# A convolution fused with a gated feed-forward layer: building the band from 16-column pieces, and another order of the first steps

## The chip, the cores and the metric

The kernel runs on one core of a Trainium2 chip. The metric is the device time of one execution in microseconds, lower being better. It is the median of several executions of the same program. One further execution was taken with the hardware profiler, and every duration of single instructions comes from that one.

## What is computed

`x` is (8, 4096, 192), the convolution's `weight` is (8, 7), one row of 7 taps for each of 8 heads of 24 columns. Each output row of the convolution is a weighted sum of the row and the six before it (zeros ahead of the first row of each of the 8 sequences), with the taps of a head passed through a softmax. The result, 32768 rows of 192, goes through a gated feed-forward layer.

```python
w = np.exp(weight - np.max(weight, axis=-1, keepdims=True))
w = w / (np.sum(w, axis=-1, keepdims=True) + 1e-09)
x_pad = np.concatenate([np.zeros((B, pad, D)), x], axis=1)      # pad = 6
idx = np.arange(S)[:, None] + np.arange(K)[None, :]             # K = 7
x_unf = x_pad[:, idx, :].reshape(B, S, K, H, group)             # H = 8, group = 24
y = np.einsum('hk,bskhg->bshg', w, x_unf).reshape(B * S, D)
g = y @ w_gate                                                  # (192, 1536)
out = (g / (1 + np.exp(-g))) * (y @ w_val) @ w_out              # (1536, 192)
```

## The kernel before

**Tiling.** The 32768 rows are cut into 64 blocks of 512 rows, and the hidden width of 1536 into 12 chunks of 128. A *step* `n` is one chunk of one block: block `b = n // 12`, chunk `j = n % 12`. There are 768 steps. Four blocks form a unit of 2048 rows, for which the convolution is made at one time.

**One step** (`gate_val`, L537): six products of 64 rows by 128 columns with 512 moving columns, three for `gate` and three for `val`. Gate products use rows 0 to 63 of the array, val products rows 64 to 127, and one of each runs beside the other. ScalarE then takes the silu of `gate` (L554) and VectorE multiplies it with `val` into `h` (L556), of which 15 buffers exist.

**Down projection** (`down`, L561; `slot`, L604). The twelve `h` of a block are multiplied by `w_out` into two accumulators, `acc0` and `acc1`. Each `h` is used by row halves, and the halves swap accumulators between a first and a second pass. The 96 products of a block are divided among four slots: slot 1 (first pass, chunks 0 to 5), slot 2 (second pass over these, then the first pass over chunks 6 to 8), slot 3 (second pass over 6 to 8, first over 9 to 11), slot 4 (second pass over 9 to 11, then the two copies out of the accumulators, L626 and L627, and the store). Slots of block `b` stand behind steps 7 and 10 of the block and 1 and 4 of the next. The first product of a slot waits for `after`, a silu of an earlier step: `silu[n - 2]`. A function `work` can be put between the parts of a slot.

**Convolution.** It is a product with a band matrix. For units from 1 on, `band` (32 rows) is used in `conv_half`; its result goes to DRAM, and blocks are read back transposed (`fetch`). For unit 0, the first four blocks, there is a separate, faster way: `early(e)` (L366) makes 64 small products with the wider band `wide`, and ScalarE and VectorE copy the result to `tme`. Blocks 0 to 2 are then turned on TensorE by `eturn` (L430), 15 transposes against the identity `ident`, and copied to the three `xc` tiles that the steps read. Block 3 takes the way over DRAM (`eout`, `efetch`).

**Constants and the band.** On POOL, `pid` holds each partition's number and `jid` (L184) the column numbers 0 to 127. VectorE makes from them `eye`, 32-column pieces of an identity, `shift`, four pieces that select rows, and, at the end of `make_wide` (L346), `ident`. The softmax of the taps gives `split`, each tap as a high and a low half in fp16. `spread_taps` (L278) brings the taps to the partitions by 16 tiny products, and multiplies them with copies of `eye` to `spread`. `make_wide` (L319) makes `wide` from `shift` and `spread` with four products of 512 columns into two banks, and four copies. `keep_warm` (L640) sends products of zeros with 512 columns through TensorE: seven ahead of the taps, two behind.

**Loads.** `x` and the weights are loaded and cast to fp16 by POOL's queue, in the order of the source: `xe` of block 0 (three loads: the first window without its 6 padding rows, the windows 1 to 5, the second row half), the weights of chunks 0 to 2 and 3 to 7 (three loads each), `xe` of block 1, the weights of chunks 8 to 11, `w_out` in two parts, `xe` of blocks 2 and 3, then `x` of unit 1.

**Order.** Every instruction is put in the order of the source on its own engine by `seq` (L72), also those on POOL that issue loads. The first turn is at L656; then the loop over the steps begins (L660). In it `early(1)` follows step 4, `eturn(1)` step 6, slot 1 of block 0 step 7, slot 2 step 10 with `early(2)` in its middle, slot 3 step 13, slot 4 step 16, `eturn(2)` step 17, and `early(3)` is in slot 1 of block 1, at step 19.

## Time and profile before

| what | value |
|---|---|
| median of three executions | 793.20 us (793.19 to 794.07) |
| the profiled execution | 793.83 us, of which its span is 792.0 us |
| TensorE products, share of the span | 99% |
| VectorE, ScalarE, POOL busy, share of the span | 74%, 66%, 9% |
| chain that ended last: TensorE's share | 97% |
| first gate product starts | 9.97 us |
| slot 1 of block 1 starts | 32.41 us |
| last product ends | 787.42 us |

A span is counted from the first instruction of the program on the core to the last one. Times in a timeline are microseconds from the span's start; the second number of a line is how long the instruction, or a group of merged ones, lasted. A bracket at the end tells how long the engine had been idle and what released it. POOL's rows for loads show the issue of a load alone; the data land later. Ends of products on TensorE are modelled, so that starts are the safer thing to compare.

The median, the profiled execution and its span differ by up to 1.2 us, so that a difference between two kernels is taken between numbers of the same kind.

### The profile page before, as it was taken

The page shows a single profiled execution, that of the slowest core. Times are in us where ns is not written, and L with a number is a line of the kernel's source. Part 1 is how long each engine was busy: PE and PEld are TensorE (multiplying, and loading weights), DVE is VectorE, ACT ScalarE, POOL GpSimd, SP SyncE. Part 2 cuts the span into 40 slices and gives each one's busy share as a digit, 9 for nine tenths or more (in the row PEclk, how much of TensorE's full clock was granted, in tenths as well). Part 3 has the DMA queues.
Part 4 walks back from the last instruction along what each step waited for, and adds up shares of the span by engine and source line. Part 5 has one row for each costly group of instructions (what it writes and reads, how often), then busy time and mean ns, then how long its engine had stood idle before and what let it go on. Part 6 is the DMA issues. An engine that isn't in the chain of part 4 may idle for free.

```text
span 792.0 us, 28590 instructions
## 1 busy us (share of the span) xinstructions
PE 784.0 (99%) x12018; PEld 493.9 (62%) x12018; DVE 584.1 (74%) x933; ACT 522.2 (66%) x910; POOL 67.4 (9%) x93
## 2 busy tenths in 40 slices
PE   8999999999999999999999999999999999999997
PEld 4666666666666666666666666666666666666665
DVE  7677777777777867767777777777777777777775
ACT  5676766666666666757666666666667667676664
POOL 8111010010100101001010000100001010000000
PEclk9999999999999999999999999999999999999999
DMA  9999577786857778567894769858587794726311
GB/s 131 149 204 146 125 116 118 164 124 146 105 120 152 129 147 119 120 126 125 155 140 113 117 112 165 128 133 118 112 154 121 150 115 118 136 81 116 80 42 42
DMA packets 214961, 99.23 MB, mean 125 GB/s; under 512 B 148776, under 2 KB 213936, under 8 KB 213936
## 3 DMA queue, kind: packets, MB, share of 16 engines
q1 hardware_dynamic: 167424, 78.75, 49.3%
q0 software_dynamic: 47136, 18.45, 21.7%
q8 instruction: 94, 1.54, 0.8%
q14 instruction: 35, 0.29, 0.1%
q10 hardware_dynamic: 272, 0.20, 0.1%
HBM read 36.90 MB, written 41.16 MB: 99 GB/s over the span
## 4 chain that ended last, share of the span: by engine, by line
PE 97%; DMA 1%; POOL 1%; DVE 0%; ACT 0%; issue 0%; POOLq 0%
PE gate L545 61%; PE acc L571 32%; PE cv L469 2%; PE val L545 1%; DMA xe<-in_x_dram 1%; POOL w L162 0%; POOL xe L97 0%; PE acc L592 0%; PE cv L380 0%; PE turn L438 0%; DVE h L556 0%; ACT sig L554 0%; DVE o_sb L627 0%; DVE tm L486 0%; ACT o_sb L731 0%
## 5 line engine op out<-in xcount | busy, mean ns | idle before, releaser
L556 DVE TENSOR_TENSOR h<-sig,val 128x512 f16<-128x512 f16 x768 | 507.7, 687 | 195.4 <-PE val L545 192.9
L554 ACT ACTIVATE sig<-gate 128x512 f16<-128x512 f32 x768 | 458.5, 597 | 234.9 <-PE val L545 207.4
L545 PE MATMUL val<-xc,w 64*128 64x512 f16 x2304 | 539.1, 376 | 0.2 <-DVE tm L486 0.2
L545 PE MATMUL gate<-xc,w 64*128 64x512 f16 x2304 | 539.2, 376 | 0.0
L545 PEld LDWEIGHTS <-w 64*128 64x128 f16 x4608 | 221.0, 94 | 212.7 <-issue 1.2
L571 PEld LDWEIGHTS <-h 64*128 64x128 f16 x6096 | 257.8, 94 | 66.0 <-issue 6.1
L571 PE MATMUL acc<-wo,h 64*128 64x192 f16 x6096 | 298.8, 243 | 0.0
L97 POOL DMA_DIRECT2D x<-in_x_dram x40 | 31.6, 792 | 437.0 <-ACT sig L554 429.9
L486 ACT CAST tm<-cv 128x480 f16<-128x480 f32 x60 | 30.6, 562 | 22.1 <-PE cv L469 22.1
L486 DVE CAST tm<-cv 128x480 f16<-128x480 f32 x60 | 36.6, 652 | 2.6
L627 DVE COPY o_sb<-acc 128x384 f32<-128x384 f32 x63 | 34.7, 550 | 0.0
L497 POOL COPY tm<-tm 128x1280 f16<-128x1280 f16 x15 | 18.8, 1252 | 137.3 <-DVE tm L486 129.1
L626 ACT COPY o_sb<-acc 128x384 f32<-128x384 f32 x63 | 30.1, 478 | 0.0
L469 PE MATMUL cv<-x,band 64*32 64x240 f16 x960 | 18.2, 265 | 0.0
L469 PEld LDWEIGHTS <-band 64*32 64x32 f16 x960 | 10.1, 91 | 4.9 <-issue 4.7
L132 POOL MEMSET x<- 6x192 f16 x7 | 1.7, 248 | 59.7 <-PE cv L469 59.6
L97 POOL DMA_DIRECT2D xe<-in_x_dram x9 | 6.0, 692 | 0.4 <-issue 0.3
L643 PE MATMUL warm<-fill 128*128 128x512 f16 x9 | 4.2, 628 | 1.2 <-DVE fill L91 1.2
L398 ACT CAST tme<-cv 128x288 f16<-128x288 f32 x8 | 2.9, 401 | 2.5 <-PE cv L380 2.5
L380 PE MATMUL cv<-xe,wide 64*64 64x48 f16 (+1 forms) x256 | 3.2, 192 | 1.1 <-ACT wide L338 0.6
L380 PEld LDWEIGHTS <-wide 64*64 64x64 f16 x256 | 2.7, 108 | 2.5 <-ACT wide L338 1.1
L438 PE MATMUL turn<-ident,tme 128*128 128x128 f16 x45 | 3.3, 220 | 0.8 <-ACT tme L398 0.5
(53 smaller groups left out, 40.0 us busy)
## 6 DMA issues: line engine op xcount, KB each, us to landing
out_dram<-o_sb SPq DMA_DIRECT2D x63, 384.0 KB
scr<-tm SPq DMA_DIRECT2D x105, 130.0 KB
x<-x SPq DMA_DIRECT2D x28, 480.0 KB
x<-in_x_dram POOLq DMA_DIRECT2D x24, 480.0 KB, 9.4
x<-in_x_dram POOLq DMA_DIRECT2D x7, 468.0 KB, 7.4
xc<-scr SPq DMA_TRANSPOSE x180
scr<-tm SPq DMA_DIRECT2D x15, 104.0 KB
wo<-in_moe_w_out_dram POOLq DMA_DIRECT2D x2, 288.0 KB, 6.3
```

The lines of the kernel that those rows point to most:

```text
L97: nc.gpsimd.dma_start(out=t[p0 + i0 : p0 + i1, w0 - at : w1 - at, :], in_=bass.AP(tensor=x_flat.tensor, offset=(t0 + size * w0 - pad + i0) ...
L380: nc.tensor.matmul(o[Q * c : Q * c + Q, at : at + w], wide[Q * r : Q * r + Q, a, h, :], xe[e][Q * r : Q * r + Q, c : 2 * G : 2, h * grp : ...
L469: nc.tensor.matmul(banks[r][32 * c : 32 * c + 32, t * w : t * w + w], band[Q * r : Q * r + Q, h, :], x16[u][Q * r : Q * r + Q, NG * c : NG ...
L486: eng(tm[u][:, NG * r : NG * r + NG, 2 * grp * hp : 2 * grp * hp + 2 * grp].rearrange("p g (t e) -> p g t e", t=2), banks[r][:, 0 : 2 * w] ...
L497: seq(nc.gpsimd.tensor_copy(tm[u][:, :, SL * Q : 4 * Q], tm[u][:, :, 0:Q]))
L545: nc.tensor.matmul(o, w16[p0 : p0 + Q, k, ts(j, P)], xc[b][k][p0 : p0 + Q, 0:TB], start=(k == 0), stop=(k == SL - 1),)
L554: silu[n] = seq(nc.scalar.activation(sg, g, AF.Silu)).ins
L556: seq(nc.vector.tensor_tensor(hj, sg, v, op=ALU.mult))
L571: nc.tensor.matmul(acc[b][bank][:, s, :], hj[p0 : p0 + Q, ts(2 * bank + s, P)], wo16[p0 : p0 + Q, j, :], start=(not second and j == 0 and ...
L626: seq(nc.scalar.copy(o_sb[:, 0:2, :], acc[b][0]))
L627: seq(nc.vector.tensor_copy(o_sb[:, 2:4, :], acc[b][1]))
L643: nc.tensor.matmul(warm, fill[:, 0:P], fill, start=True, stop=True, skip_group_check=True,)
```

## The change

**Constants.** `jid` is replaced by `jn`, four rows of 64 numbers, `i - 16 n`. A new tile `cid` holds the column numbers 0 to 127 and is read by `ident` alone; its iota stands on POOL behind the last load of `w_gate` and `w_val`. The pieces are 16 columns wide instead of 32. `shift` is made in two operations instead of four.

**Band.** With 16-column pieces all 8 taps (7 and the small one) fit on 128 partitions. `spread_taps` takes two products instead of 16, and one multiplication instead of two. `make_wide` takes four products of 256 columns, each on its own, instead of four of 512 that add in pairs. The products of zeros behind the taps are five of 128 columns instead of two of 512.

**First rows of x.** The windows 1 to 5 of block 0 are loaded first; window 0 follows with 56 rows instead of 58. All 64 rows of window 0 are set to zero ahead of this.

**Order of steps.** `early(1)` follows step 5, `eturn(1)` step 7. Slots 1, 2 and 3 of block 0 follow steps 9, 11 and 13 and wait for `silu[n - 1]`; `early(2)` is in slot 2 at step 11. `eturn(2)` follows step 18. Slot 4 of block 0 and all that follows are where they were.

```diff
             if e == 0 and r == 0:
-                windows(xe[e], 0, 0, EO, 0, 1, i0=pad)
                 windows(xe[e], 0, 0, EO, 1, w1)
+                windows(xe[e], 0, 0, EO, 0, 1, i0=pad, i1=Q - 2)
...
-    jid = small("jid", [P, P], i32)
-    seq(nc.gpsimd.iota(jid, pattern=[[1, P]], base=0, channel_multiplier=0))
+    jn = small("jn", [P, 4, Q], i32)
+    seq(nc.gpsimd.iota(jn, pattern=[[-16, 4], [1, Q]], base=0, channel_multiplier=0))
     xe_tile(0)
-    seq(nc.vector.memset(xe[0][0:pad, 0, :], 0.0))
+    seq(nc.vector.memset(xe[0][0:Q, 0, :], 0.0))
     xe_load(0)
     load_w(0, 384)
     load_w(384, 1024)
     xe_tile(1)
     xe_load(1)
     load_w(1024, Dff)
+    cid = small("cid", [P, P], i32)
+    seq(nc.gpsimd.iota(cid, pattern=[[1, P]], base=0, channel_multiplier=0))
     load_wo(0, 6)
...
+    def make_shift(n):
+        seq(
+            nc.vector.tensor_tensor(
+                shift[:, n : n + 2],
+                jn[:, n : n + 2].unsqueeze(2).to_broadcast([P, 2, 2, Q]),
+                both.unsqueeze(2).unsqueeze(3).to_broadcast([P, 2, 2, Q]),
+                op=ALU.is_equal,
+            )
+        )
...
+        for a in range(2):
+            seq(
+                nc.tensor.matmul(
+                    bank[:, a * H : a * H + H],
+                    split[:, a].rearrange("h k q -> h (k q)"),
+                    eye[0:H, 0:H],
+                    start=(a == 0),
+                    stop=True,
+                    skip_group_check=True,
+                )
+            )
...
+        for n in range(4):
+            c0 = 16 * 2 * H * (n % 2)
+            seq(
+                nc.tensor.matmul(
+                    banks[n // 2][:, c0 : c0 + 16 * 2 * H],
+                    shift[:, n].rearrange("p r i -> p (r i)"),
+                    spread.rearrange("p j a h -> p (j a h)"),
+                    start=(n % 2 == 0),
+                    stop=True,
+                    skip_group_check=True,
+                )
+            )
...
             nc.vector.tensor_scalar(
-                ident, jf, scalar1=pf, scalar2=None, op0=ALU.is_equal
+                ident, cid, scalar1=pf, scalar2=None, op0=ALU.is_equal
             )
...
     keep_warm(7)
     spread_taps()
-    keep_warm(2)
+    keep_warm(5, P)
     make_wide()
...
+        if n == 5:
+            early(1, (*acc_banks, gate_bank))
+        elif n == 7:
+            eturn(1, (*acc_banks, gate_bank))
+        elif n in (9, 11):
+            slot(1 if n == 9 else 2, b, silu[n - 1], work)
+        elif n == 13:
+            slot(3, 0, silu[n - 1])
+        elif j % 3 == 1 and b:
+            k = {1: 3, 4: 4, 7: 1, 10: 2}[j]
+            slot(k, b - 1 if j < 7 else b, silu[n - 2], work if j > 4 else None)
+            if j == 4 and work:
+                work()
+        if n == 18:
+            eturn(2, (*acc_banks, gate_bank))
+        elif n == 20:
+            eout(3)
+        elif n == 21:
+            efetch(3)
```

## The prediction, made before the changed kernel was run

> **What bounds the kernel now.** I read the page's engine totals, then the busy times by stretch, then the chain of waits and the timelines of single engines over the first 35 us, where every edit of the change lies.

> ```profile
> PE 784.0 (99%) x12018; PEld 493.9 (62%) x12018; DVE 584.1 (74%) x933; ACT 522.2 (66%) x910; POOL 67.4 (9%) x93
> ```

> TensorE carries the time. The stretches are: head, start-up steps, the rest in two pieces.

> ```profile
> 1.20:9.97 8.77, 7.71 (x109) 3.46 (x110) 6.27 (x29) 4.93 (x10) 8.34 (x14) 1.00 0.82 97
> 9.97:32.41 22.44, 21.53 (x377) 13.32 (x376) 15.85 (x28) 14.47 (x27) 9.74 (x16) 1.00 1.57 183
> 60.00:787.40 727.40, 727.40 (x11048) 459.56 (x11044) 540.68 (x842) 483.37 (x840) 45.26 (x54) 1.00 0.69 123
> ```

> After 60 us TensorE has no gap at all and the change touches nothing there. So the end moves only by what happens before 32.41, where slot 1 of block 1 begins: by then both orders have done the same work. Two sums decide: when the first gate product starts (9.97 now), and what is lost between it and that point.

> The lost part: 20 steps of 6 products at 0.6465 (a free run of 18 takes 1.94) are 12.93, two early convolutions of 64 products at 0.67 are 1.34, two turns of 15 transposes at 0.94 are 1.88, 96 down products at 0.0413 are 3.96; together 20.11. The stretch takes 22.44, so 2.33 is lost. From the chain of waits (first three lines) and TensorE's timeline:

> ```profile
> 7.55 6.91 DMA xe<-in_x_dram
> 29.85 0.56 DVE o_sb L627
> 30.45 0.72 PE turn L438 x10
> ```
> ```profile
> 12.23 0.21 PEld L545 LDWEIGHTS <-w 64*128 64x128 f16 x4 [0.29 <-DMA w<-in_moe_w_val_dram]
> 14.50 0.72 PE L380 MATMUL cv<-xe,wide 64*64 64x48 f16 x63 [0.56 <-DMA xe<-in_x_dram]
> ```

> The reader sees three waits: step 3 for weights that landed at 12.19 (0.37), the early convolution of block 1 for its x, which landed at 14.46 (0.76), and the turn of block 2 for an accumulator bank being emptied (0.51). The remaining 0.7 is the second product pair waiting for its xc (0.15) and drains of 0.1 to 0.15 wherever products change shape.

> What sets the first gate: POOL's and DVE's own order.

> ```profile
> 0.94 0.22 POOL L184 IOTA jid<- 128x128 int32 x1
> 9.68 0.54 POOL L162 DMA_DIRECT2D w<-in_moe_w_val_dram  x1 [0.21 <-issue]
> 11.64 1.68 POOL L172 DMA_DIRECT2D wo<-in_moe_w_out_dram  x2 [1.42 <-DMA w<-in_moe_w_gate_dram]
> ```
> ```profile
> 7.04 0.76 DVE L338 CAST wide<-taps 128x256 f16<-128x256 f32 x2 [1.27 <-PE taps L326]
> 7.72 0.28 DVE L346 TENSOR_SCALAR ident<-jf,pf 128x128 f16<-128x128 f32 x1
> 8.47 0.56 DVE L398 CAST tme<-cv 128x384 f16<-128x384 f32 x1 [0.48 <-PE cv L380]
> 9.41 0.43 DVE L443 COPY xc<-turn 128x520 f16<-128x520 f16 x1
> ```
> ```profile
> 5.43 1.58 PE L326 MATMUL taps<-spread,shift 128*128 128x512 f16 x4
> 7.57 0.83 PE L380 MATMUL cv<-xe,wide 64*64 64x72 f16 x64 [0.56 <-ACT wide L338]
> 8.89 1.14 PE L438 MATMUL turn<-ident,tme 128*128 128x128 f16 x15 [0.50 <-ACT tme L398]
> ```

> POOL issues 14 loads without a pause to speak of, about 0.63 each, until 10.22. The 14th waited for the landing of the 6th (issued 4.65, landing in 4.8, so 9.4; the issue follows at 9.68), the 15th for the 7th. ident stands on DVE ahead of block 0's tme copy, and the turn needs both.

> [...] each order is that of the source. [...] So an iota behind loads is not complete before them; the trace shows no iota there, but the band copy on POOL starts only at 20.26, as the load ahead ends. [...] The trace has the half clock at the start (512-column warm products 0.427 apart, later 0.215)[...].

> **The change part by part.**

> *Band.* Sixteen tap products become two (0.29 to about 0.1), two 512-column warm products become five of 128 (0.83 to 0.53 at 0.107, the half-clock spacing), four 512-column products become four of 256 (the first three 0.42 apart; now 0.213, 0.85 in all), spread one operation instead of two. Tap products still follow the seventh warm product (its columns end at 4.17). From the last tap product to the first big one took 0.93 (4.50 to 5.43); less 0.2 for the smaller spread, the big ones begin at 5.0, the fourth at 5.65. From fourth to DVE's wide copy 0.42, from there to early(0) 0.53: early(0) at 6.6, done at 7.4, some 1.0 earlier. The equality on integers with two broadcasts (256 columns) is not in the trace: two 128-column ones take 0.4 start to start; between that and double, it hides under the warm products. Fewer constant operations on DVE likewise. I cost all of this at nothing, because of the next item; without that cover it is worth up to 1.0 at the first gate.

> *cid.* ident no longer reads the iota from 0.94 but cid, queued on POOL behind 14 loads. jn is twice as wide as jid (one column 0.12, 128 columns 0.22: so 0.32), moving the loads by 0.1; starting with the bulk of x and ending with 56 rows may bring the 6th landing forward by up to 0.5, but POOL's own issue then holds: the 14th ends at 10.1 to 10.3, cid at 10.3 to 10.5. I take 10.4. DVE starts ident at 10.45, and behind ident wait block 0's tme copy, its wrap copy and both xc copies, for which TensorE waits in order. From ident's start to the tme copy 0.25 at least (its own 0.28, overlapping a little), and from tme's start to the first gate 1.50 now (8.47 to 9.97). First gate: 10.45 + 0.25 + 1.50 = 12.2, 2.2 later.

> *Memset of 64 rows, window 0 after the bulk.* Memset is off the path (over by 1.24, the load at 2.2); x of block 0 landed by 5.7 and early(0) needs it at 6.6. Nothing.

> *Order of steps.* Starting at 12.2, no weights are late: step 3 comes at 14.2 (landed 12.58), step 8 near 19.3 (16.03), slot 1 near 20.6 (19.14). Early(1) after step 5 comes at 16.3, with x there since 14.46: 0.37 and 0.76 go. eturn(2) moved one step on, to n = 18, finds the accumulators nearly empty: 0.51 becomes about 0.15. What is added: slots 1 to 3 of block 0, two steps apart, wait for silu[n-1] instead of silu[n-2]. The row of three silus at 20.13 (1.89) shows the price: step 8 starts at 19.29, so silu starts 0.84 after its step and ends at 1.44; two steps on the slot is ready at 1.29. With the semaphore 0.2 each; bounded below by 0 if no wait shows and above by 0.4 if weights must be loaded afresh. Behind the waiting product stand only TensorE's own; ACT and DVE run dry no sooner. I take 0.22, so 0.66. Losses: 0.15 xc, 0.1 early(1), 0.1 turn, 0.66, 0.15 early(2), 0.15 turn of 2, 0.1 slot 1 of block 1: 1.4.

> Sum: 12.2 + 20.11 + 1.4 = 33.7 against 32.41: 1.3 later. The profiled execution (793.83, of which 1.83 lies outside its span of 792.0) would become 795.1; it is 0.63 above the median of 793.2, so I put 1.3 on the median: 794.5. The loads of later units, the stores on SP and conv from step 28 move with it; their slack (unit 1's x landed at 34.31, used at 43.06) is larger.

> **Rivals.**

> *Clock falls back.* TensorE idles from 7.4 to 10.8, then does 1.4 of small transposes: [...] Price: [...] 3.0 later, 796.2[...].

> *Slots wait longer* (0.6 each, ACT behind with copies): 1.1 more, 795.6. Against: ACT has 0.4 to 1.2 idle before these silus in the trace.

> *Not slower: ident is not late.* If cid completes by about 9.0 (POOL not held by the loads), the first gate comes by 10.8, and with the 1.3 or so of saved waits the change breaks even; earlier still, weights hold step 3 and x holds early(1) to 14.50 again, but with one more step done. Then 15.17 + 14 steps 9.05 + turns 1.88 + down 3.96 + early(2) 0.67 + losses 1.25 = 32.0: 0.4 earlier, 792.8. Against: both queues are in order in every row.

> **How the numbers follow.** Forecast 0.48, clock 0.34, slots 0.07, not slower 0.11. What can be told from no change is 0.2%, 1.6 us: up to 794.8. The forecast alone spans 794.0 to 795.3 (first gate 12.0 to 12.5, slot waits 0.1 to 0.4) and passes the bound in a third of its cases: slower 0.16 + 0.34 + 0.06 = 0.56, faster 0.03, within 0.41. Range 793.4 to 796.8: it leaves out the deeper clock cases and most of the not-slower one.

> **What would show it.** cid on POOL after 10; ident on DVE idle until then, released by POOL; turn after 10.7; first gate near 12.2; no wait of early(1) for x; three waits of about 0.2 for ACT before down products; the turn of block 2 without a wait for o_sb. Wrong if ident stands near 7, or if gate pairs after 12.2 come 0.43 apart.

## The result, and the profile after

The changed kernel takes 797.03 us (797.00 to 797.13, four executions) beside 793.20 (792.92 to 794.07) of the kernel before: a ratio of 1.0047, 95% interval 1.0029 to 1.0064. The profiled execution took 797.02, with a span of 795.2. The forecast of 794.5 was too low, and its range of 793.4 to 796.8 ended 0.2 short.

The page's engine totals, and the same stretches as before, ended at the same work (first gate product; slot 1 of block 1; 60 us; last product). Columns: stretch and its length, busy us and count of each engine, granted clock, DMA share, GB/s.

```profile
PE 784.8 (99%) x12007; PEld 494.0 (62%) x12007; DVE 583.0 (73%) x928; ACT 522.3 (66%) x910; POOL 67.9 (9%) x94
```
```profile
1.20:12.49 11.29, 7.19 (x98) 4.09 (x99) 5.09 (x24) 4.81 (x10) 10.36 (x18) 0.82 0.95 123
12.49:35.24 22.75, 22.64 (x376) 12.79 (x376) 16.09 (x28) 14.47 (x27) 8.06 (x14) 0.94 1.40 155
60.00:790.45 730.45, 730.45 (x11090) 461.49 (x11086) 543.67 (x847) 486.00 (x845) 45.37 (x54) 1.00 0.67 123
```

The first gate product comes 2.52 later than before (12.49 against 9.97). Slot 1 of block 1 comes 2.83 later (35.24 against 32.41) and the last product 3.03 later (790.45 against 787.42). After 60 us TensorE again has no gap, so everything lies in the first 40 us. What is new is the clock column: 0.82 and 0.94 in the first two stretches, where it was 1.00. (The column leaves out the half clock ahead of a program's first rise: before, it has 1.00 from 1.20 on, though the first products of zeros are 0.427 apart and later ones 0.215.)

POOL's timeline, then VectorE's, then TensorE's, of the changed kernel:

```profile
8.80 1.19 POOL L162 DMA_DIRECT2D w<-in_moe_w_val_dram  x2
9.94 0.31 POOL L194 IOTA cid<- 128x128 int32 x1
11.05 1.67 POOL L172 DMA_DIRECT2D wo<-in_moe_w_out_dram  x2 [0.81 <-DMA w<-in_moe_w_gate_dram]
```
```profile
5.74 0.76 DVE L323 CAST wide<-taps 128x256 f16<-128x256 f32 x2 [0.62 <-PE taps L310]
10.29 0.28 DVE L331 TENSOR_SCALAR ident<-cid,pf 128x128 f16<-128x128 int32 x1 [3.79 <-POOL cid L194]
10.49 0.55 DVE L383 CAST tme<-cv 128x384 f16<-128x384 f32 x1
11.53 0.43 DVE L428 COPY xc<-turn 128x520 f16<-128x520 f16 x1
```
```profile
6.27 0.83 PE L365 MATMUL cv<-xe,wide 64*64 64x72 f16 x64 [0.56 <-ACT wide L323]
10.62 1.93 PE L423 MATMUL turn<-ident,tme 128*128 128x128 f16 x15 [3.53 <-DVE ident L331]
12.49 0.60 PE L530 MATMUL gate<-xc,w 64*128 64x512 f16 x1
12.89 0.63 PE L530 MATMUL gate<-xc,w 64*128 64x512 f16 x1
13.31 0.63 PE L530 MATMUL gate<-xc,w 64*128 64x512 f16 x1
15.30 0.38 PE L530 MATMUL gate<-xc,w 64*128 64x512 f16 x1
15.52 0.38 PE L530 MATMUL gate<-xc,w 64*128 64x512 f16 x1
18.03 0.73 PE L365 MATMUL cv<-xe,wide 64*64 64x72 f16 x64
```

cid is made as soon as the fourteenth load is issued, ident follows at 10.29 after 3.79 of idle on VectorE, and TensorE idles for 3.53. That is the late identity that was foreseen. The second cost shows in the starts of the gate products (some rows are left out of the cut): 0.40 to 0.43 apart up to 15.0, and 0.22 after it. The first six steps, up to the early convolution at 18.03, take 5.55. The turn, too, takes 1.87 to the first gate product instead of 1.07; with the same late ident at full clock it takes 1.27 (below), so that 0.6 of this is the clock. Windows of 3.41 us, cut at the clock's changes (4.90, 8.32, 15.14) and halfway between the last two, say why:

```profile
4.90:8.30 3.40, 1.63 (x71) 1.21 (x69) 0.98 (x4) 1.35 (x4) 3.40 (x7) 1.00 1.04 126
8.32:11.73 3.41, 1.11 (x10) 0.85 (x10) 1.21 (x4) 0.00 (x0) 2.60 (x5) 0.50 1.28 184
11.73:15.14 3.41, 3.41 (x22) 1.76 (x22) 1.18 (x3) 1.19 (x2) 3.41 (x6) 0.50 1.36 192
```

The clock rose at 4.90 and fell again at 8.32, when TensorE had been idle for 1.2 only since the early convolution, after a window in which it was busy for 1.63 of 3.40. It stayed at half until a full window (11.73 to 15.14) had been busy.

The waits that the new order adds are of the size foreseen: the weight load of a slot of block 0 waits for the silu of the step before. In the timeline of weight loads:

```profile
22.55 0.94 PEld L556 LDWEIGHTS <-h 64*128 64x128 f16 x24 [0.53 <-ACT sig L539]
25.04 0.94 PEld L556 LDWEIGHTS <-h 64*128 64x128 f16 x24 [0.53 <-ACT sig L539]
28.80 0.94 PEld L556 LDWEIGHTS <-h 64*128 64x128 f16 x24 [0.53 <-ACT sig L539]
```

The two steps ahead of each take 1.50 from start to start instead of 1.29, so each wait costs TensorE 0.21, less than the 0.53 for which the weight loads stand idle.

### The profile page after: what moved, and what is told of

Its sections match the earlier page's. It is cut to its first block, busy times and chain, and to the rows that moved or that the text cites. A ratio compares the mean times of both kernels' runs of the same rounds, so it can differ in the third digit from the quotient of the medians.

```text
span 795.2 us, 28566 instructions
## 1 busy us (share of the span) xinstructions
PE 784.8 (99%) x12007; PEld 494.0 (62%) x12007; DVE 583.0 (73%) x928; ACT 522.3 (66%) x910; POOL 67.9 (9%) x94
## 4 chain that ended last, share of the span: by engine, by line
PE 98%; POOL 1%; DVE 0%; ACT 0%; issue 0%; POOLq 0%
PE gate L530 61%; PE acc L556 32%; PE cv L454 2%; PE val L530 1%; POOL w L162 1%; PE turn L423 0%; POOL xe L97 0%; PE acc L577 0%; PE cv L365 0%; DVE h L541 0%; ACT sig L539 0%; DVE tm L471 0%; ACT o_sb L710 0%; DVE o_sb L612 0%; POOL jn L184 0%
## 5 line engine op out<-in xcount | busy, mean ns | idle before, releaser
L454 PEld LDWEIGHTS <-band 64*32 64x32 f16 x960 | 10.1, 91 | 4.9 <-issue 4.7
L423 PEld LDWEIGHTS <-tme 128*128 128x128 f16 x45 | 3.2, 111 | 4.7 <-issue 3.8
L628 PE MATMUL warm<-fill 128*128 128x512 f16 (+1 forms) x12 | 3.8, 490 | 1.2 <-DVE fill L91 1.2
L428 ACT COPY xc<-turn 128x520 f16<-128x520 f16 x3 | 1.8, 592 | 4.7 <-PE turn L423 4.5
```

What stands on the lines that cost most here:

```text
L423: nc.tensor.transpose(bank[:, g, :], tme[b][:, g, Q * k : Q * k + P], ident)
L454: nc.tensor.matmul(banks[r][32 * c : 32 * c + 32, t * w : t * w + w], band[Q * r : Q * r + Q, h, :], x16[u][Q * r : Q * r + Q, NG * c : NG ...
```

## The experiments

Theory 1: ident waits for cid, and the idle that this makes costs the clock as well. Theory 2: the loss is in the new order of steps and its waits for the silu just before, and ident only moves the head.

### cid's iota behind the sixth load

```diff
     load_w(0, 384)
+    cid = small("cid", [P, P], i32)
+    seq(nc.gpsimd.iota(cid, pattern=[[1, P]], base=0, channel_multiplier=0))
     load_w(384, 1024)
...
     load_w(1024, Dff)
-    cid = small("cid", [P, P], i32)
-    seq(nc.gpsimd.iota(cid, pattern=[[1, P]], base=0, channel_multiplier=0))
```

> The changed kernel with the iota of cid put behind the sixth load on POOL instead of the fourteenth. Theory 1 (ident waits for cid, and the idle that this makes costs the clock as well): ident is made before 7.0, the turn starts near 7.6, the first gate product near 8.7, no half clock after 6; step 3 then waits for its weights (landed at 10.8 to 12.0), and slot 1 of block 1 starts at 31.0 instead of 35.2, so the time is about 792.0, 1.2 below the kernel before and 5 below the changed one. Theory 2 (the loss is in the new order of steps and its waits for silu[n-1]; ident only moves the head): the head gets shorter, but the time stays above that of the kernel before, 794 or more.

Measured: 793.12 (792.65 to 795.52) beside 793.51, ratio 0.9997 (0.9990 to 1.0004). VectorE's timeline and the window after the clock's rise, in this version's profile (792.71):

```profile
6.41 0.28 DVE L331 TENSOR_SCALAR ident<-cid,pf 128x128 f16<-128x128 int32 x1
7.17 0.56 DVE L383 CAST tme<-cv 128x384 f16<-128x384 f32 x1 [0.48 <-PE cv L365]
```
```profile
4.85:8.25 3.40, 2.31 (x83) 1.76 (x82) 2.18 (x8) 1.42 (x4) 3.40 (x7) 1.00 1.13 127
```

ident is there at 6.41, the first gate product at 8.59, slot 1 of block 1 at 30.85, all as Theory 1 has it; the window is 68% busy and the clock stays. So the place of one iota accounts for the whole loss. Theory 2 falls: the new order is in here. The median, however, is 1.1 above what was expected: the single executions spread over 2.9, and the profiled one was among the shortest.

### The idle filled with products of zeros

```diff
     early(0, (gate_bank, gate_bank, val_bank))
+    busy = ppool.tile([P, TB], fp32, tag="val", name="busy")
+    for _ in range(14):
+        seq(
+            nc.tensor.matmul(
+                busy, fill[:, 0:P], fill, start=True, stop=True,
+                skip_group_check=True,
+            )
+        )
```

> The changed kernel with 14 products of zeros with 512 columns behind the early convolution of block 0, in the 3.5 us in which TensorE waits for ident. Theory 1: they keep the clock at full speed; ident still comes at 10.3, but the turn takes 1.1 instead of 1.9 and the first six steps 4.1 instead of 5.55: 2.0 to 2.2 less, 794.9. Rival (the slow first steps come from loads that share memory with TensorE's reads, not from the clock): products of zeros change nothing, 797.0.

Measured: 795.37 (795.33 to 796.62), ratio 1.0026 (1.0015 to 1.0037) to the kernel before, 1.7 below the changed one. Work was added and time fell. The execution of 796.62 was the profiled one: there the clock rose only at 10.43, the fourteen products took 4.3 instead of 3.0 (14 times 0.215), and the turn began at 12.11, after ident (10.27):

```profile
7.78 4.49 PE L644 MATMUL busy<-fill 128*128 128x512 f16 x14
12.11 1.00 PE L423 MATMUL turn<-ident,tme 128*128 128x128 f16 x15
```

Eight products instead of fourteen end before ident where the clock is up by then:

> The changed kernel with 8 products of zeros in its idle instead of 14, so that they end before ident even at half clock (8 times 0.43 is 3.4). Theory 1: the turn starts at 10.6 as in the changed kernel, and if the clock stays up, the turn takes 1.0 and the first six steps 4.2: the end comes 2.0 earlier, 795.1. If 8 leave too much of a window idle, the clock falls as in the changed kernel: 797. Rival (products of zeros help by something other than the clock): less time even where the record shows half clock.

Measured: eight executions in two groups, which the mean granted clock of each separates: 795.29, 795.31, 795.36 and 795.42 at 0.999; 796.70, 796.74, 796.76 and 796.83 at 0.997. This is the clearest price of the clock: one program, 1.4 apart. The step of 0.002 is about what one of the changed kernel's windows of 3.41 at half clock makes in 795 (an estimate: 1.7 / 795). No profile of the second group was kept, so the place of its fall is not shown; the profile is from the first group. TensorE's timeline, and the window that holds ident's wait:

```profile
10.60 1.31 PE L423 MATMUL turn<-ident,tme 128*128 128x128 f16 x15 [1.26 <-DVE ident L331]
11.87 0.37 PE L530 MATMUL gate<-xc,w 64*128 64x512 f16 x1
12.31 0.37 PE L530 MATMUL gate<-xc,w 64*128 64x512 f16 x1
12.53 0.37 PE L530 MATMUL gate<-xc,w 64*128 64x512 f16 x1
16.34 0.73 PE L365 MATMUL cv<-xe,wide 64*64 64x72 f16 x64
```
```profile
9.70:13.10 3.40, 2.31 (x25) 1.48 (x26) 1.87 (x5) 0.75 (x2) 2.31 (x5) 1.00 1.33 184
```

The turn starts as in the changed kernel (10.60), but the first gate product comes at 11.87 instead of 12.49, the six steps take 4.46 instead of 5.55, and slot 1 of block 1 starts at 33.54 instead of 35.24. So where the clock is kept, the late ident leaves 1.8 over the kernel before (795.35 to 793.54). Nothing speaks for the rival of loads that disturb TensorE's reads: the two groups are one program with the same loads, and products of zeros take none away.

### The late cid alone, and the order alone, in the kernel before

```diff
     load_w(1024, Dff)
+    cid = small("cid", [P, P], i32)
+    seq(nc.gpsimd.iota(cid, pattern=[[1, P]], base=0, channel_multiplier=0))
...
-                ident, jf, scalar1=pf, scalar2=None, op0=ALU.is_equal
+                ident, cid, scalar1=pf, scalar2=None, op0=ALU.is_equal
```

> The kernel before with one edit of the change: ident reads a cid whose iota stands behind the fourteenth load. Theory 1: ident at 10.4 and the first gate product at 12.3 to 12.5; the waits of step 3 for weights and of the early convolution of block 1 for x (1.1 together) go, so 1.2 to 1.4 slower at full clock, 794.5, and up to 3.2 slower if the clock falls here too (early convolution later, at 7.6 to 8.4, so the idle is 2.3 and not 3.5: I expect full clock). Theory 2: under 0.5 slower, 793.5.

Measured: 796.97 (796.54 to 797.64), ratio 1.0045 (1.0032 to 1.0057). One edit gives, within the noise, the whole result of the change. My expectation of a full clock was wrong in the same way as the forecast. TensorE's timeline, then the windows:

```profile
10.87 1.31 PE L440 MATMUL turn<-ident,tme 128*128 128x128 f16 x15 [2.95 <-DVE ident L348]
12.14 0.37 PE L547 MATMUL gate<-xc,w 64*128 64x512 f16 x1
```
```profile
5.58:8.99 3.41, 1.78 (x69) 1.02 (x67) 0.95 (x4) 1.42 (x4) 3.41 (x7) 1.00 1.11 144
8.99:12.40 3.41, 1.39 (x17) 0.95 (x17) 1.62 (x5) 0.46 (x1) 2.02 (x4) 1.00 1.17 159
12.40:15.80 3.40, 3.35 (x18) 1.40 (x17) 1.20 (x3) 1.32 (x3) 3.39 (x6) 0.50 1.33 175
```

The turn ran at full clock (10.87 to 12.14, again 1.27), and the clock fell just as the steps began, after a window that was 41% busy; five steps took 5.15 instead of 3.23.

The order alone puts the new step loop into the kernel before:

> The kernel before with the new order of steps alone. Theory 1: the early convolution of block 1 hides its wait for x behind one more step (0.65 gained), the turn of block 2 meets empty banks (0.4 gained), three slots wait 0.2 each and slot 1 of block 1 a little (0.8 lost): 0.2 to 0.4 faster, 792.9. Theory 2: 1 or more slower, 794.2.

Measured: 793.28 (792.62 to 793.74) beside 793.51, ratio 0.9998 (0.9990 to 1.0006): no difference that can be told. In its profile slot 1 of block 1 starts at 31.82; in the two profiles of the kernel before it is at 32.41 and 31.84.

### The band alone, and the turn of block 2 alone

The version with cid early and the old order of steps has the new band, constants and loads:

> The band, the constants and the loads of the changed kernel with cid's iota behind the sixth load, in the old order of steps. Theory 1 (the shorter head is cut off by the loads: step 3 cannot start its val products before its weights, landed at 11.3 to 11.7, nor the early convolution of block 1 before its x at 13.6): the first gate product at 8.6, slot 1 of block 1 at 31.2 to 31.5, so about 1.0 below the kernel before, 792.4. Rival (the 16-column band itself costs later, by its one-sided products or its fewer products of zeros): equal to or above the kernel before, 793.5 or more.

Measured: 794.48 (793.23 to 796.31), ratio 1.0008 (1.0000 to 1.0017). I expected 792.4. By the number alone this is the result of the rival, a band that costs later; but the same band in the new order took 793.12 (cid's iota behind the sixth load, above). The profiled execution was the longest, 796.31. TensorE's timeline, then the windows:

```profile
14.55 0.19 PE L365 MATMUL cv<-xe,wide 64*64 64x72 f16 x1 [1.19 <-DMA xe<-in_x_dram]
15.18 0.67 PE L365 MATMUL cv<-xe,wide 64*64 64x48 f16 x35 [0.44 <-DMA xe<-in_x_dram]
```
```profile
11.91:15.31 3.40, 1.77 (x27) 0.68 (x31) 1.69 (x3) 1.19 (x2) 2.25 (x4) 1.00 1.34 190
15.33:18.73 3.40, 3.40 (x75) 1.52 (x67) 1.59 (x3) 1.39 (x3) 3.40 (x6) 0.50 1.58 188
```

The steps start at 8.59 but x of block 1 landed at 14.5 and 15.1 here, so the early convolution waits 1.63 in two pieces, the window is 52% busy, and the clock falls. The same version in another execution:

> The version with the new band and cid early in the old order, once more. Its first profile (796.3) had the early convolution of block 1 waiting for x until 15.18 and half clock after it. Theory: where x lands earlier, the clock stays up and the time is near 793.5; where it lands late, the clock falls and it is 795 or more.

```profile
13.42 1.01 PE L365 MATMUL cv<-xe,wide 64*64 64x72 f16 x64 [0.83 <-DMA xe<-in_x_dram]
```

It took 793.60: x landed at 13.38 and 13.67, the wait was 0.94 (0.83 and 0.11 within the group), and the clock stayed up. Slot 1 of block 1 started at 31.63. So in the old order a head that is ready 0.6 to 1.4 earlier is given back as a longer wait for x, and in the profile in which x was late, the longer wait took the clock too. Not every long execution can be put down to a fall: of the seven over 794, three (794.88, 795.03, 795.14) have a mean clock of 0.999, like the short ones. Why x lands at 13.4 in one execution and 14.5 in another was not tried.

The new order is thus worth nothing in the kernel before, but something with the early ident: its early convolution comes one step later and hardly waits for x (0.03 in the profile), and three of its 21 executions are over 794, against seven of 13 in the old order (medians 793.12 and 794.48).

The turn of block 2 one step later, in the kernel before:

> The kernel before with the turn of block 2 one step later (step 18), nothing else. Theory 1: the 0.51 that the turn waits for an accumulator bank go, slot 1 of block 1 waits 0.2 to 0.3 for the turn's copies instead: 0.2 to 0.3 faster, 793.3 beside 793.5. Rival: the wait only moves, no difference.

Measured: 793.26 (792.46 to 793.84) beside 793.57, ratio 0.9996 (0.9987 to 1.0004). The 0.51 of the turn's wait is gone in its profile (0.94 from the first transpose to the next step) and slot 1 of block 1 takes 0.79 instead of 0.59 for its first part. The gain of 0.3 is the expected one, but the interval does not part it from nothing.

### Gaps closed, slots spaced

```diff
     make_wide()
+    keep_up(1)
     early(0, (gate_bank, gate_bank, val_bank))
+    keep_up(1)
```

`keep_up(1)` is one 512-column product of zeros into a spare val bank; cid stands behind the sixth load.

> The changed kernel with cid's iota behind the sixth load, and one product of zeros in each of the two gaps of 0.5 around the early convolution of block 0. If the spread of the version without them (792.65 to 795.52) comes from the clock rising late or falling in some executions, the slow ones go: all of them within 792.4 to 793.2, median 792.6. If it comes from the landing of the loads, the spread stays and the median with it, 793.1.

Measured: 793.04 (792.65 to 794.14), ratio 0.9993 (0.9985 to 1.0001). The median is nearly that of the version without these products (793.12), so the clock does not explain the bulk of the spread. The long executions beyond 794.2 are gone, but that is none of 13 where there were three of 21, which can be chance; and those three had a mean clock of 0.999, like the short ones. A late rise in them, which this mean leaves out, would fit and is not shown. The longest of the thirteen, which is the profiled one, has a single stop of 0.56 at 77.4 us with no wait that the profile shows; what it was stays open.

Then the slots are spaced, on top of this (the condition that skips the old place of slot 4 is left out of the cut):

```diff
-        elif n in (9, 11):
-            slot(1 if n == 9 else 2, b, silu[n - 1], work)
-        elif n == 13:
-            slot(3, 0, silu[n - 1])
+        elif n in (8, 11):
+            slot(1 if n == 8 else 2, b, silu[n - 2], work)
+        elif n == 14:
+            slot(3, 0, silu[n - 2])
+        elif n == 16:
+            slot(4, 0, silu[n - 1])
```

> The one before with slots 1 to 3 of block 0 behind steps 8, 11 and 14, each three steps apart and so waiting for silu[n-2], and slot 4 behind step 16 with silu[n-1]. Theory 1: three waits of 0.21 become one: 0.4 below the one before, 792.2. Rival (the waits are hidden, since loads bound this stage): no difference.

Measured: 792.59 (791.84 to 793.64) beside 793.54, ratio 0.9988 (0.9981 to 0.9994): faster than the kernel before by 0.12%, and by the medians 0.56% below the changed one. The median is 0.45 below that of the version with the two products of zeros, and 19 of the 21 executions are below that version's median; so the gain is there, near the 0.4 expected. The profiles show only 0.16 of it from the early convolution of block 1 to step 24 (23.34 against 23.50): three waits of 0.20 become one, which is 0.40 less, but slot 1 takes 1.13 instead of 1.00 from its first product to the next step, slot 2 1.14 instead of 1.09 to the early convolution in its middle, and the early convolution of block 1 waits 0.06 more for x.

### The kernel before once more

> The kernel before once more, for a second profile. If its spread (792.7 to 794.3) comes from when the loads land, slot 1 of block 1 starts earlier or later than 32.41 by as much as the waits of step 3 for weights and of the early convolution of block 1 for x are shorter or longer, and everything after 60 us is alike. If it comes from elsewhere, that start is 32.4 whatever the time.

```profile
13.72 0.93 PE L380 MATMUL cv<-xe,wide 64*64 64x72 f16 x64 [0.21 <-DMA xe<-in_x_dram]
```

It took 793.37 against 793.83 in the first profile. The first gate product came at 9.32 instead of 9.97, because the clock had risen at 5.36 instead of 6.54; but the early convolution of block 1 waits for x in both. x of block 1 landed at 13.89 instead of 14.46, slot 1 of block 1 started at 31.84 instead of 32.41, and the last product ended 0.56 earlier, at 786.86. By these two profiles the kernel before moves with the landing of its loads; the profile that the forecast was worked from was a late one.

## Why the prediction was wrong

*Late ident: held.* cid was done at 10.25 (10.4 foreseen), ident began at 10.29 (10.45), tme's copy at 10.49 (10.7). The late cid by itself, in the kernel before, gives a ratio of 1.0045.

*Band and first loads hidden: held.* early(0) began at 6.27 (6.6 foreseen). The sixth load landed at 8.83 instead of 9.40. POOL's own issue (the fourteenth load's ended at 9.99, cid's iota began at 9.94) held cid, as worked out.

*From tme's copy to the first gate, 1.50: failed.* It was 2.00, since the turn ran at half clock; in the version with eight products, at full clock, it is 1.41. This is 0.5 of error, of which an earlier ident gave back 0.2: 12.49 for 12.2.

*Losses of 1.4 from there to slot 1 of block 1: failed.* They were 2.64 (22.75 less 20.11). Term by term: the first six steps lost 1.67 where 0.15 and a drain of 0.1 were put; of the excess 1.1 is half clock (5.55 less the 4.46 with eight products), and 0.3 is there at full clock too and was not foreseen; the three slots lost 0.62 (0.66 foreseen); the drains ahead of the two turns and of early(2) 0.30 (0.40); the waits of step 3 for weights and of early(1) for x are gone, as foreseen. Past that point slot 1 of block 1 takes 0.29 more than its products (0.1 foreseen for it).

*The step that failed* is in the rivals: "Clock falls back" was put behind the forecast with 0.34. That weight was my estimate; the trace of the kernel before shows no fall ahead of its last product (787.42). In the changed kernel the clock fell with 48% of the window busy (4.90 to 8.32) and only 1.2 of idle just before it, and in the late-cid version with 41% (8.99 to 12.40), the transposes among the busy part. By the windows of 3.41 measured here, the question to ask was whether about half of one would be idle, and the idle that was foreseen, 3.4 us from 7.4 to 10.8, leaves about that in one window or the next, however they lie. The price was right. The rival's 3.0 less the forecast's 1.3 leaves 1.7 for the clock: slot 1 of block 1 starts 1.70 later than in the version with eight products at full clock (0.62 up to the first gate product, 1.08 in the first six steps), and the medians of the changed kernel and of the one with fourteen products differ by 1.7. Without the fall the sum would have held: with eight products slot 1 of block 1 starts at 33.54, where the forecast has 33.7. That it is so close is in part luck, since the first gate product came 0.3 earlier than 12.2 and the first six steps lost 0.3 more.

*The base: mis-sized.* The sum was 1.3 on a profiled execution and was carried to the median unchanged. That execution lay 0.63 over the median of 793.20. About half of this was a low median of few executions: the 17 to 44 taken beside the experiments have 793.51 to 793.57. The rest goes with loads that landed late in it (slot 1 of block 1 at 31.84 in the other profile, which took 793.37). The changed kernel waits for an identity that POOL's issue sets, and its four executions agree within 0.13. A difference of 3.2 between profiles is thus 3.8 between the first medians, and 3.5 against 793.5; with the 0.63 even the rival's 796.2 is 796.8.

## What to carry to other kernels

A constant that one early instruction needs belongs ahead of the loads on a queue that issues in order, as POOL's does in these traces, or at least ahead of the one that ends near its use: with cid behind the fourteenth load ident began at 10.29 and the kernel took 797.03, with cid behind the sixth 6.41 and 793.12. Count an idle of TensorE twice: once as time (3.53 ahead of the turn in the changed kernel), and once for what runs at half clock after it (1.70 there). In these profiles the clock fell after windows of 3.41 us that were busy for 41, 48 and 52%, and stayed after others busy for 52, 68 and 69%. And where one kernel waits for loads and the other does not, don't carry a difference of single profiled executions over to medians without a second profile of the one that waits. An order of steps that is worth nothing in one head (793.28 beside 793.51 in the kernel before) can be worth something in an earlier one (793.12 beside 794.48 with cid early).

## What the runs showed of the hardware that was not expected

```
window                     busy   clock after it
before 6.54 to 9.95        0.69   stays
cid early 4.84 to 8.25     0.68   stays
8 products 9.71 to 13.13   0.68   stays
late cid 5.58 to 8.99      0.52   stays
cid early, old order
        11.91 to 15.32     0.52   falls
changed 4.90 to 8.32       0.48   falls
late cid 8.99 to 12.41     0.41   falls
```

In these seven the border lies near half of a window (0.52 is on both sides); whether the clock goes by just this share is not shown. If it does, transposes count as work, by an estimate from these windows: in the third line they are some 1.1 of the 2.3 busy, and without them that window would be 35% busy and the first line's 38%, both below the 48% that lost the clock without a transpose in it.
